# Mixing matmuls of an attention and gated-MLP kernel on float16 pairs in place of float32r pairs

## The chip, the cores and the metric

The kernel runs on one core of one Trainium2 chip. The metric is device time in microseconds for one launch. Before the change it is 624.42 us, the median of three runs (623.97 to 627.14).

The core has five engines that run their own instruction streams and meet at semaphores: TensorE (PE, with the weight loads shown apart as PEld), VectorE (DVE), ScalarE (ACT), GpSimd (POOL) and SyncE (SP), which issues the DMAs here.

## The reference

Two stages follow each other. The attention is causal with a window of 128, with a linear bias for each head; its heads are joined into x. The MLP splits its hidden layer in halves u and v, normalises v over its features, mixes v over the sequence with `w_spatial`, and multiplies the result into u.

```
B, H, S, D = 8, 8, 576, 64          # x: 8 x 576 x 512
scores = q @ k.T / sqrt(D) - slope[h] * |i - j|, kept where 0 <= i - j < 128
x = softmax(scores) @ v              # heads side by side
h = relu(x @ w_in)                   # 512 -> 1024
u, v = h[..., :512], h[..., 512:]
v_n = (v - mean(v)) / sqrt(var(v) + 1e-6)
v_s[b, t, d] = sum_s w_spatial[t, s] * v_n[b, s, d] + b_spatial[t]
out = (u * v_s) @ w_out              # 512 -> 512
```

`w_spatial` is 576 x 576 with normally distributed entries of size 0.64 / 576, and `b_spatial` lies around 1. All inputs and the output are float32.

## The kernel before

The work is held to 128 partitions. The sequence of 576 is four tiles of 128 and a rest of 64. Products that must be more exact than one pass are done on pairs: an operand is a high part plus a low part, and three matmuls add high x high, high x low and low x high (`PASS`).

For each of eight batches the attention makes x in four pairs of heads: scores on PE (L537), a fused bias and row minimum on VectorE (L548), the exponential on ACT (L554), then a split of the scaled probabilities into float16 high and low parts on ACT and VectorE (L589, L594), a DMA transpose, and float16 matmuls with v (L656). Some pairs at the start take another road with full float32 matmuls (`raw_tile`, `raw_rest`).

The MLP of a batch is made of units, each filling one PSUM tile `m`, of which there are two. Five v units (L721, and L743 for the rest of 64) make v: relu, `layer_norm`, then a split into `vn`, high and low. Eight u units (L773) make u transposed, relu'd. Eight mixing units (`sp_unit`, L794) multiply `vn` with the pairs `wsp` of the transposed mixing weights: twelve matmuls on whole tiles and two on the rest, where `l1`, `l2`, `r1`, `r2` hold the rest's high and low parts stacked, with the bias in two further rows. VectorE then multiplies the PSUM tile into u (L802), and the product is split again (`gs`). Eight output units (L820) multiply with `wout` and go out by DMA. The string `UORDER` sets the order of these kinds in a batch.

The order of the instructions on each engine is made by a planner (`Plan`). Every operation has an engine, a weight, a due time and the parts of buffers that it reads and writes; an `either` operation has two engines to choose from, and the planner takes the one that it reckons to be free first. Operations that are ready go out by due time. Because all engines share one plan, an added operation can move others and change which of ACT and VectorE gets an `either`. `copy` (L278) and `relu` (L282, L283) are such helpers, so their operations stand under the helper's line.

At the start the weights are prepared between the first batch's attention tiles: `win` and `wout` are split from float64 words by bit operations (`split_w64`, L297 to L335), and the mixing weights are split from float32 by `wsp_weights` (L365 to L373) and `rest_weights` (L382 to L404). The latter load into buffers `gs`, of which there are five; the splits of `win` use the same five for their steps.

Of the kernel before, what the change touches and what calls it, by code (L numbers as in the profile page):

```python
# [140 lines left out]
def attn_gmlp_kernel(ctx, tc, qk, v, w_in, w_spT, b_sp, w_out, outT):  # L141
# [14 lines left out]
    PSC = 4096.0  # L156
    VORDER = (0, 4, 1, 2, 3)
# [203 lines left out]
    def wsp_weights(c, due):  # L361
        st = plan.buf(work, "gs", 5, [P, S], F32)

        def f():
            nc.sync.dma_start(st(), w_spT[c * P:(c + 1) * P, :])  # L365
        plan.add("SP", dma(P * S * 4), due - 4000, f, (), [(st, 0)])

        def f():
            nc.scalar.copy(wsp()[:, c, 0, :], st())
        plan.add("ACT", act(S), due, f, [(st, 0)], [(wsp, (c, 0))])  # L370

        def f():
            nc.vector.tensor_tensor(wsp()[:, c, 1, :], st(), wsp()[:, c, 0, :].bitcast(F32), ALU.subtract)  # L373
        plan.add("DVE", dve(S), due, f, [(st, 0), (wsp, (c, 0))], [(wsp, (c, 1))])

    def rest_weights(due):
# [474 lines left out]
    for c in range(NQ - 1):  # L851
        wsp_weights(c, FIRST + 8000 + 2000 * c)
# [64 lines left out]
```

## Time and profile before

| | |
|---|---|
| time, median of three runs | 624.42 us (623.97 to 627.14) |
| span of the profiled execution | 625.2 us |
| mean granted TensorE clock | 0.985 |
| matmuls | 5388 |
| VectorE instructions counted | 1945 |
| ACT instructions counted | 1312 |

The page gives the span as the only time of the profiled execution; it is 0.8 us above the median and lies inside the runs. "Busy" counts the time in which at least one instruction of an engine was under way. Matmuls overlap their neighbours, so a matmul's mean is a latency and not its share of the time. A group names line, engine, operation, tiles written and read, shapes and count; then busy microseconds and mean nanoseconds of one; then the idle time just before its instructions, with what ended it. `x0`, `vn0` and the like lose their numbers in the views, so `m` stands for both PSUM tiles.

### The profile page before, as it was taken

What the parts mean: (1) busy time and instruction counts of PE and PEld (TensorE: products, weight loads), DVE (VectorE), ACT (ScalarE), POOL (GpSimd) and SP (SyncE); (2) the same over time, 40 slices, a digit from 0 to 9 for tenths busy, and PEclk for the clock granted to TensorE, in tenths of its full rate; (3) what the DMA queues carried; (4) which work ended last, traced back from release to release, by engine and by line L of the source; (5) the groups of instructions that cost most, each with busy time, mean ns of one, the idle gap of its engine ahead of it and who ended that gap; (6) DMA issues with size and microseconds to landing.
All of it is one profiled execution on the core that took longest, in us unless ns stands there. A gap on an engine that the chain in (4) does not pass through costs nothing. (4 is left out here: it accounts for less than half of the span.)

```text
span 625.2 us, 14903 instructions
## 1 busy us (share of the span) xinstructions
PE 591.6 (95%) x5388; PEld 521.6 (83%) x5388; DVE 536.7 (86%) x1945; ACT 422.7 (68%) x1312; POOL 30.0 (5%) x53
## 2 busy tenths in 40 slices
PE   4889899799899998999999999999999999999997
PEld 2446579689689987998899988998899889998997
DVE  7989888998998988998999999999999899984532
ACT  4678765897785775975597677877597568752211
POOL 1000010000100001000100001000200010000100
PEclk9979799989999999999999999999999999999999
DMA  7902113499746681587646872587557761671001
GB/s 262 348 23 86 63 68 102 136 187 218 148 100 140 145 206 60 116 151 181 140 120 121 190 171 81 121 190 174 127 116 157 176 118 35 93 140 45 0 23 54
DMA packets 153613, 80.27 MB, mean 128 GB/s; under 512 B 132930, under 2 KB 144194, under 8 KB 153540
## 3 DMA queue, kind: packets, MB, share of 16 engines
q1 hardware_dynamic: 153540, 79.32, 54.0%
q8 instruction: 42, 0.69, 0.5%
q14 instruction: 31, 0.25, 0.1%
HBM read 37.13 MB, written 9.44 MB: 74 GB/s over the span
## 5 line engine op out<-in xcount | busy, mean ns | idle before, releaser
L554 ACT ACTIVATE prob<-prob,stat 128x256 f32<-128x256 f32 (+2 forms) x270 | 125.3, 466 | 36.7 <-DVE stat L548 36.7
L794 PE MATMUL m<-wsp,vn 128*128 128x288 f32 x768 | 122.2, 299 | 3.8 <-DVE u L802 1.7
L773 PE MATMUL m<-xt,win 128*128 128x288 f32 x768 | 111.6, 298 | 4.2 <-DVE u L283 2.2
L794 PEld LDWEIGHTS m<-wsp,vn 128*128 128x128 f32 x768 | 107.0, 188 | 8.6 <-DVE u L802 2.8
L773 PEld LDWEIGHTS m<-xt,win 128*128 128x128 f32 x768 | 103.9, 188 | 9.5 <-DVE u L283 3.9
L820 PE MATMUL m<-gs,wout 128*128 128x288 f32 x768 | 110.3, 299 | 0.2 <-ACT o L278 0.2
L589 ACT ACTIVATE pq<-prob,stat 128x128 f16<-128x128 f32 x270 | 104.4, 466 | 7.4 <-ACT prob L554 2.4
L820 PEld LDWEIGHTS m<-gs,wout 128*128 128x128 f32 x768 | 103.5, 189 | 4.1 <-DVE gs L808 1.5
L594 DVE SCALAR_TENSOR_TENSOR pq<-prob,stat,pq 128x128 f16<-128x128 f32 x270 | 104.9, 435 | 1.7 <-ACT pq L589 0.9
L721 PE MATMUL m<-win,xt 128*128 128x512 f32 x384 | 92.9, 397 | 2.4 <-DVE vt L283 1.7
L721 PEld LDWEIGHTS m<-win,xt 128*128 128x128 f32 x384 | 72.3, 190 | 19.5 <-DVE vt L283 2.1
L548 DVE CUSTOM_DVE_ANT_0 prob<-s,tab 128x256 f32<-128x256 f32 (+2 forms) x222 | 75.0, 377 | 1.0
L691 POOL TENSOR_TENSOR st<-st,nhalf 128x1 f32<-128x1 f32 (+1 forms) x40 | 26.0, 652 | 538.1 <-DVE st L687 527.2
L554 ACT ACTIVATION_READ_ACCUMULATOR prob<-prob,stat 128x1 f32 (+1 forms) x270 | 50.8, 188 | 0.0
L802 DVE TENSOR_TENSOR u<-m,u 128x288 f32<-128x288 f32 x64 | 28.6, 449 | 25.5 <-PE m L794 25.1
L537 PE MATMUL s<-qkraw 64*64 64x192 f32 (+2 forms) x876 | 41.9, 316 | 2.9 <-DVE stat L548 2.9
L656 PE MATMUL x<-pt,vh 128*64 128x256 f16 (+6 forms) x756 | 42.0, 229 | 0.0
L537 PEld LDWEIGHTS s<-qkraw 64*64 64x64 f32 x876 | 30.9, 136 | 9.6 <-issue 4.8
L282 ACT ACTIVATE vt<-m 128x512 f32<-128x512 f32 x31 | 18.5, 595 | 27.8 <-DVE st L686 17.3
L656 PEld LDWEIGHTS <-vh 128*64 128x64 f16 x756 | 32.3, 110 | 4.8 <-issue 4.6
L656 PE MATMUL x<-pt,vl 128*64 128x256 f16 (+6 forms) x378 | 35.5, 228 | 0.0
L278 ACT COPY o<-m 128x288 f32<-128x288 f32 x36 | 14.1, 393 | 31.7 <-PE m L820 24.1
(132 smaller groups left out, 837.3 us busy)
## 6 DMA issues: line engine op xcount, KB each, us to landing
qkraw<-in_qk_dram SPq DMA_DIRECT2D x28, 576.0 KB, 4.2
out_dram<-o SPq DMA_DIRECT2D x64, 144.0 KB, 2.1
vraw<-in_v_dram SPq DMA_DIRECT2D x28, 320.0 KB, 3.0
vn<-in_w_in_dram SPq DMA_DIRECT2D x6, 512.0 KB, 6.8
pt<-in_w_out_dram SPq DMA_DIRECT2D x4, 512.0 KB, 4.3
gs<-in_w_spT_dram SPq DMA_DIRECT2D x4, 288.0 KB, 4.9
xt<-in_w_in_dram SPq DMA_DIRECT2D x2, 512.0 KB, 7.0
qkraw<-in_qk_dram SPq DMA_DIRECT2D x3, 320.0 KB, 9.0
```

What stands on the lines that cost most here:

```text
L537: nc.tensor.matmul(sc[k][j]()[out, i, a - k0:z - k0], raw()[rows, 0, q:q + D], raw()[rows, 1, a:z], start=True, stop=True, skip_group_chec ...
L548: nc.vector.tensor_tensor_reduce(pt(), sc()[:m, i, :n], tabs[h]()[:m, c0:c0 + n], -0.125, 3e38, ALU.add, ALU.min, st()[:m, NM, j, t:t + 1])
L554: nc.scalar.activation(pt(), pt(), AF.Exp, bias=st()[:m, NM, j, t:t + 1], scale=-1.0, accum_out=st()[:m, SM, j, t:t + 1])
L589: nc.scalar.activation(pq[j]()[:m, 0, cs], prob[j]()[:m, cs], AF.Copy, scale=st()[:m, RC, j, t:t + 1])
L594: nc.vector.scalar_tensor_tensor(pq[j]()[:m, 1, cs], prob[j]()[:m, cs], st()[:m, RC, j, t:t + 1], pq[j]()[:m, 0, cs], ALU.mult, ALU.subtract)
L656: nc.tensor.matmul(xp()[j * D:(j + 1) * D, x0:x0 + n], l()[:, kt, j * D:(j + 1) * D], rhs[:, o:o + n], start=j not in seen, stop=False, sk ...
L691: nc.gpsimd.tensor_tensor(st()[:m, 11:12], st()[:m, 10:11], nhalf()[:m], ALU.pow)
L721: nc.tensor.matmul(pt(), xt[c]()[:, X0[a] + t * P:X0[a] + (t + 1) * P], win()[:, c, w, DH:DF], start=(n == 0), stop=(n == 3 * NC_ - 1))
L773: nc.tensor.matmul(pt()[:, :HS], win()[:, c, w, d * P:(d + 1) * P], xt[c]()[:, X0[a] + hf * HS:X0[a] + (hf + 1) * HS], start=(n == 0), sto ...
L794: nc.tensor.matmul(pt()[:, :HS], l, r, start=(n == 0), stop=(n == len(ops) - 1))
L802: nc.vector.tensor_tensor(u(), pt()[:, :HS], u(), ALU.mult)
L820: nc.tensor.matmul(pt()[:, :HS], wout()[:, d, w, e * P:(e + 1) * P], gs[d]()[:, a, :], start=(n == 0), stop=(n == 3 * ND - 1))
```

## The change

Three groups of things change.

First, the tiles `wsp`, `r1`, `r2`, `l1`, `l2` and `vn` become float16. The pairs stay pairs: high part rounded to float16, low part the rounded remainder, and the same three products. The tile `vn` keeps its size in bytes, since the loads of `w_in` pass through it. PE's mixing matmuls read float16 on both sides.

Second, factors keep the float16 values in range. `layer_norm` multiplies the variance by 2048 to the power of -2, so v_n comes out 2048 times as large. The mixing weights and the bias are multiplied by a power of two that is found on the device from the largest row sum of absolute values: ACT takes absolute values of all weights with a running sum a partition, VectorE takes the largest of three sums, spreads it over 128 columns as bfloat16, a DMA transposes that, and `scale_of` reduces it and works on the exponent bits. The factor that undoes both goes into the gating multiply, which becomes `scalar_tensor_tensor`.

Third, the loads of the mixing weights go to a tile of their own, `wraw`, and `mixing_weights` takes the place of `rest_weights` and `wsp_weights`, with one due time of 8000 after `FIRST`. The splits read the factor, so they come after the scan.

```diff
+    VSC = 2048.0
-    wsp = fixed([P, NQ - 1, 2, S], F32R, "wsp")
-    r1 = fixed([P, S], F32R, "r1")
-    r2 = fixed([P, S], F32R, "r2")
-    l2 = fixed([P, DH], F32R, "l2")
+    wsp = fixed([P, NQ - 1, 2, S], F16, "wsp")
+    wraw = fixed([P, NQ - 1, S], F32, "wraw")
+    wam = fixed([P, 8], F32, "wam")
+    r1 = fixed([P, S], F16, "r1")
+    r2 = fixed([P, S], F16, "r2")
+    l2 = fixed([P, DH], F16, "l2")
...
+        for c in range(NQ - 1):
+            plan.add("SP", dma(P * S * 4), due - 4000 + c, lambda c=c: nc.sync.dma_start(wraw()[:, c, :], w_spT[c * P:(c + 1) * P, :]),
+                     (), [(wraw, c)])
...
+        def f():
+            nc.scalar.activation(flat(), wraw(), AF.Abs, accum_out=wam()[:, 0:1])
+            nc.scalar.activation(r1(), rs(), AF.Abs, accum_out=wam()[:, 1:2])
+            nc.scalar.activation(r2()[64:65], bt()[64:65], AF.Abs, accum_out=wam()[64:65, 2:3])
+        plan.add("ACT", act((NQ + 1) * S, 1) + 400, due, f, chunks + [(rs, 0), (bt, 0), (wam, 0), (r2, 2)],
+                 [(wsp, (c, 0)) for c in range(NQ - 1)] + [(wam, 1), (r1, 0), (r2, 1)])
...
+        def f():
+            nc.vector.tensor_reduce(wam()[:, 3:4], wam()[:, 0:3], AX.X, ALU.max)
+            nc.vector.tensor_copy(wide(0), wam()[:, 3:4].to_broadcast([P, P]))
+        plan.add("DVE", 300, due + 1, f, [(wam, 1)], small[0] + [(wam, 2)])
+        plan.add("SP", 300, due + 2, lambda: nc.sync.dma_start_transpose(out=wide(1), in_=wide(0)), small[0], small[1])
...
+            scale_of(wam, wide(1), 2.0 ** -13 / VSC)
...
+                nc.scalar.activation(wsp()[:, c, 0, :], wraw()[:, c, :], AF.Copy, scale=sc())
...
+                nc.vector.scalar_tensor_tensor(wsp()[:, c, 1, :], wraw()[:, c, :], sc(), wsp()[:, c, 0, :], ALU.mult, ALU.subtract)
...
+    def scale_of(am, rows, back):
+        bits = 0x7F800000
+        nc.vector.tensor_reduce(am()[:, 1:2], rows, AX.X, ALU.max)
+        nc.vector.tensor_scalar(am()[:, 2:3], am()[:, 1:2], 2.0 ** -98, 2.0 ** 126, ALU.max, ALU.min)
+        nc.vector.tensor_scalar(am()[:, 2:3].bitcast(I32), am()[:, 2:3].bitcast(I32), bits, None, ALU.bitwise_and)
+        nc.vector.tensor_scalar(am()[:, 5:6], am()[:, 2:3], 2.0 ** -12, None, ALU.mult)
+        nc.vector.tensor_scalar(am()[:, 6:7], am()[:, 2:3], back, None, ALU.mult)
+        nc.vector.tensor_scalar(am()[:, 5:6].bitcast(I32), am()[:, 5:6].bitcast(I32), bits, None, ALU.bitwise_xor)
...
-            nc.vector.tensor_scalar(st()[:m, 10:11], st()[:m, 9:10], 1e-6, None, ALU.add)
+            nc.vector.tensor_scalar(st()[:m, 10:11], st()[:m, 9:10], 1e-6, VSC ** -2, ALU.add, ALU.mult)
...
-        vn = [plan.buf(work, f"vn{t}", 1, [P, 2, DH], F32R) for t in range(NQ - 1)]
-        l1 = plan.buf(work, "l1", 1, [P, DH], F32R)
+        vn = [plan.buf(work, f"vn{t}", 1, [P, 2, 2 * DH], F16) for t in range(NQ - 1)]
+        l1 = plan.buf(work, "l1", 1, [P, DH], F16)
...
-                nc.vector.tensor_tensor(u(), pt()[:, :HS], u(), ALU.mult)
-            plan.add("DVE", dve(HS), due, f, [(pt, 0), (u, 0)], [(u, 0)])
+                nc.vector.scalar_tensor_tensor(u(), pt()[:, :HS], wam()[:, 6:7], u(), ALU.mult, ALU.mult)
+            plan.add("DVE", dve(HS), due, f, [(pt, 0), (u, 0), (wam, 3)], [(u, 0)])
...
-    rest_weights(FIRST + 6000)
-    for c in range(NQ - 1):
-        wsp_weights(c, FIRST + 8000 + 2000 * c)
+    mixing_weights(FIRST + 8000)
```

How this moves instructions shows at three places. The rows give line, operation, tiles and shape; lines of the changed kernel are 3 to 36 higher than the same lines before. `ISA` is the fused bias and row minimum of a score tile, `prob` the probabilities, `win` the split weights, `r` and `l` the rest's tiles.

On VectorE, in the start, the rest's and the first chunk's low parts stood singly between score tiles before:

```order
L447 ISA prob_88,rstat<-s_67,tab_78 128x256
L447 ISA rstat 128x1
L474 TENSOR_SCALAR prob_88<-prob_88,rstat 128x256
L447 ISA prob_87,rstat<-s_68,tab_79 128x256
L447 ISA rstat 128x1
L393 TENSOR_TENSOR r_85<-gs,r_84 64x576
L373 TENSOR_TENSOR wsp<-gs,wsp 128x576
L278 COPY pq_89<-m 128x512
L447 ISA prob_88,rstat<-s_69,tab_80 128x256
L447 ISA rstat 128x1
```

Now the reduction of the scan and the cast stand a few score tiles later, with four scalings of `prob` on VectorE behind them:

```order
L483 ISA prob_89,rstat<-s_68,tab_75 128x256
L483 ISA rstat 128x1
L399 TENSOR_REDUCE wam<-wam 128x1
L400 CAST wsp<-wam 128x128
L494 TENSOR_SCALAR rstat<-rstat 128x2x2
L495 RECIPROCAL rstat<-rstat 128x2x2
L510 TENSOR_SCALAR prob_89<-prob_89,rstat 128x256
L510 TENSOR_SCALAR prob_90<-prob_90,rstat 128x256
L510 TENSOR_SCALAR prob_89<-prob_89,rstat 128x256
L510 TENSOR_SCALAR prob_90<-prob_90,rstat 128x256
```

The reduction L399 waits for ACT's scan, and all that follows in VectorE's queue stands behind it. `scale_of` (L437 to L442) comes some twenty operations later, and the low parts of the weights behind that.

On ACT the scan is three activations in one place, between exponentials (`prob,rstat`):

```order
L488 ACTIVATE prob_90,rstat<-prob_90,rstat 128x256
L281 COPY pq_92<-m 128x512
L390 ACTIVATE wsp,wam<-wraw 128x4x576
L391 ACTIVATE r_86,wam<-gs 128x576
L392 ACTIVATE r_87,wam<-gs 1x576
L488 ACTIVATE prob_90,rstat<-prob_90,rstat 128x256
```

Before, the casts of the mixing weights stood singly among other work:

```order
L452 ACTIVATE prob_88,rstat<-prob_88,rstat 128x256
L452 ACTIVATE prob_87,rstat<-prob_87,rstat 128x256
L369 CAST wsp<-gs 128x576
L278 CAST xt<-x 128x128
L473 ACTIVATE prob_88<-prob_88,rstat 128x256
L369 CAST wsp<-gs 128x576
```

The scan holds ACT from its first activation to its last, and the exponentials of later score tiles come after it.

On SP, which issues the loads, the mixing weights stood behind a `w_in` load, in `gs` buffers:

```order
L356 DMA pt<-in_w_out_dram 128x1024
L343 DMA vn_254<-in_w_in_dram 128x1024
L382 DMA gs<-in_w_spT_dram 64x576
L383 DMA gs<-in_w_spT_dram 64x576
L384 DMA gs<-in_b_sp_dram 1x576
L385 DMA gs<-in_b_sp_dram 1x576
L365 DMA gs<-in_w_spT_dram 128x576
L343 DMA vn_272<-in_w_in_dram 128x1024
L365 DMA gs<-in_w_spT_dram 128x576 x3
```

Now they stand ahead of the `w_out` and `w_in` loads, and a transpose is new:

```order
L369 DMA wraw<-in_w_spT_dram 128x576 x4
L359 DMA pt<-in_w_out_dram 128x1024
L346 DMA vn_261<-in_w_in_dram 128x1024
L374 DMA gs<-in_w_spT_dram 64x576
L375 DMA gs<-in_w_spT_dram 64x576
L376 DMA gs<-in_b_sp_dram 1x576
L377 DMA gs<-in_b_sp_dram 1x576
L346 DMA vn_277<-in_w_in_dram 128x1024
L402 DMA_TRANSPOSE wsp<-wsp 128x128
```

The rest and the bias kept their place and their `gs` buffers. On PE the order of the units is the same from the middle of the first batch's mixing on.

More of the change, by code (lines that the diff above doesn't have):

```diff
@@ L359, in wout_weights, with mixing_weights @@
         split_w64((st, DM), (wout, (c,)), tmp, lambda: wout()[:, c, 0, :], lambda: wout()[:, c, 1, :], due, WPE[2])
[L361 to L376, printed above, removed]
+    def mixing_weights(due):
         rs, bt = (plan.buf(work, "gs", 5, [P, S], F32) for _ in range(2))
+        chunks = [(wraw, c) for c in range(NQ - 1)]
+        for c in range(NQ - 1):
+            plan.add("SP", dma(P * S * 4), due - 4000 + c, lambda c=c: nc.sync.dma_start(wraw()[:, c, :], w_spT[c * P:(c + 1) * P, :]),
+                     (), [(wraw, c)])
         def f():
@@ L385, in f @@
             nc.sync.dma_start(bt()[96:97, :], b_sp)
-        plan.add("SP", 2000, due - 4000, f, (), [(rs, 0), (bt, 0)])
+        plan.add("SP", 2000, due - 3900, f, (), [(rs, 0), (bt, 0)])
         def f():
-            nc.scalar.copy(r1(), rs())
-        plan.add("ACT", act(S), due, f, [(rs, 0)], [(r1, 0)])
-        def f():
-            nc.vector.tensor_tensor(r2()[0:R, :], rs()[0:R, :], r1()[0:R, :].bitcast(F32), ALU.subtract)
-        plan.add("DVE", dve(S), due, f, [(rs, 0), (r1, 0)], [(r2, 0)])
+            nc.gpsimd.memset(wam(), 0.0)
+            nc.gpsimd.memset(r2()[R:P, :], 0.0)
+            nc.gpsimd.memset(l2()[R:P, :], VSC)
@@ new lines, in mixing_weights @@
+        plan.add("POOL", 1500, 0, f, (), [(wam, 0), (r2, 2), (l2, 1)])
+        flat = lambda: wsp()[:, :, 0, :]
+        def f():
+            nc.scalar.activation(flat(), wraw(), AF.Abs, accum_out=wam()[:, 0:1])
[3 more added lines that the diff above has]
+                 [(wsp, (c, 0)) for c in range(NQ - 1)] + [(wam, 1), (r1, 0), (r2, 1)])
@@ L396, in f @@
+        wide = lambda k: wsp()[:, 1 + k, 1, 0:P].bitcast(BF16)
+        small = [[(wsp, (1 + k, 1))] for k in range(2)]
         def f():
-            nc.gpsimd.memset(r2()[R:P, :].bitcast(F32), 0.0)
-            nc.gpsimd.memset(l2()[R:P, :].bitcast(F32), 1.0)
-        plan.add("POOL", 1500, due, f, (), [(r2, 2), (l2, 1)])
+            nc.vector.tensor_reduce(wam()[:, 3:4], wam()[:, 0:3], AX.X, ALU.max)
+            nc.vector.tensor_copy(wide(0), wam()[:, 3:4].to_broadcast([P, P]))
+        plan.add("DVE", 300, due + 1, f, [(wam, 1)], small[0] + [(wam, 2)])
@@ new lines, in mixing_weights, with f @@
+        plan.add("DVE", 600, due + 3, f, [(wam, 2), *small[1], (powers, 0)], [(wam, 3)])
+        sc = lambda a=0, z=P: wam()[a:z, 5:6]
+        ready = [(wam, 3)]
+        for c in range(NQ - 1):
+            def f(c=c):
+                nc.scalar.activation(wsp()[:, c, 0, :], wraw()[:, c, :], AF.Copy, scale=sc())
+            plan.add("ACT", act(S, 1), due + 10 + c * 500, f, [(wraw, c)] + ready, [(wsp, (c, 0))])
+            def f(c=c):
+                nc.vector.scalar_tensor_tensor(wsp()[:, c, 1, :], wraw()[:, c, :], sc(), wsp()[:, c, 0, :], ALU.mult, ALU.subtract)
+            plan.add("DVE", dve(S), due + 20 + c * 500, f, [(wraw, c), (wsp, (c, 0))] + ready, [(wsp, (c, 1))])
@@ L761, in f @@
             def f():
[L762 removed]
+                nc.vector.tensor_tensor(l1()[R:2 * R], vt()[0:R], l1()[0:R], ALU.subtract)
             plan.add("DVE", dve(DH), due + 6, f, [(vt, 0), (l1, 0)], [(l1, 1)])
```

18 lines of the change are left out of this document (11 added, 7 removed).

## The prediction

> **What bounds the kernel now.** I read the page's first part, then the stages, then the waits of each engine in one steady batch, then the order of time around one mixing unit.
>
> ```profile
> PE 591.6 (95%) x5388; PEld 521.6 (83%) x5388; DVE 536.7 (86%) x1945; ACT 422.7 (68%) x1312; POOL 30.0 (5%) x53
> ```
>
> These means hide the stages. Columns of the next view: stretch, length, busy time of PE, PEld, DVE, ACT and POOL, granted clock, DMA share, GB/s.
>
> ```profile
> 22.00:50.00 28.00, 23.44 (x166) 13.91 (x165) 25.12 (x99) 21.34 (x69) 0.00 (x0) 0.88 0.38 119
> 50.00:98.00 48.00, 45.09 (x277) 33.15 (x278) 44.17 (x143) 37.19 (x109) 3.90 (x5) 0.93 0.21 71
> 98.00:154.00 56.00, 51.36 (x554) 45.82 (x553) 49.14 (x198) 43.09 (x147) 1.00 (x2) 0.97 0.71 167
> 154.00:226.00 72.00, 69.20 (x673) 61.89 (x672) 66.07 (x247) 54.71 (x172) 2.78 (x5) 1.00 0.65 148
> ...
> 298.00:366.00 68.00, 67.63 (x675) 62.25 (x675) 64.31 (x238) 50.71 (x162) 3.25 (x5) 1.00 0.65 147
> ...
> 502.00:568.00 66.00, 65.64 (x636) 60.48 (x635) 57.17 (x203) 43.77 (x134) 3.25 (x5) 1.00 0.53 94
> 568.00:625.20 57.20, 53.93 (x364) 51.18 (x363) 22.64 (x55) 11.14 (x24) 2.83 (x5) 0.99 0.08 27
> ```
>
> There are three regimes. Up to 98 us VectorE is the fuller of the two elementwise engines and nearly full itself: from 22 to 98 us it idles 2.9 + 3.8 = 6.7 us. From 98 to 502 us PE and VectorE are both nearly full. From 502 us on VectorE has room and PE alone sets the pace. PE's busy time counts overlapping ends, so for the middle regime I ask who waits: PE from 226 to 568 us, then VectorE in one batch, 298 to 366 us (total us, times, longest).
>
> ```profile
> PE m L773 <- DVE u L283: 2.2, 5, 0.7
> PE m L794 <- ACT o L278: 1.7, 2, 0.9
> PE m L773 <- ACT vt L282: 1.7, 2, 1.1
> PE m L721 <- DVE o L278: 0.6, 1, 0.6
> ```
>
> ```profile
> DVE stat L577 <- ACT prob L554: 0.6, 3, 0.2
> DVE vt L752 <- ACT vt L278: 0.4, 1, 0.4
> DVE u L802 <- PE m L794: 0.4, 1, 0.4
> DVE prob L548 <- PE x L537: 0.3, 1, 0.3
> DVE st L682 <- ACT vt L282: 0.2, 1, 0.2
> ```
>
> PE waits 6.2 us in 342: it sets the pace. But VectorE waits only 1.9 us in 68, and of these 1.3 trace back to PE (0.4 and 0.3 directly, 0.4 and 0.2 through ACT's copy out of a PE tile); the other 0.6 is a loop between VectorE and ACT. So the second engine stands about one microsecond behind the first in every batch, and what is taken from PE soon meets it.
>
> **The change part by part.** *The mixing matmuls.* There are 768 + 128 = 896, 112 in a batch:
>
> ```profile
> L794 PEld LDWEIGHTS m<-wsp,vn 128*128 128x128 f32 x768 | 107.0, 188 | 8.6 <-DVE u L802 2.8 <-ACT o L278 2.1 <-issue 1.4
> ...
> L794 PEld LDWEIGHTS m<-r,l 128*128 128x128 f32 x128 | 20.5, 188 | 0.0
> ```
>
> Each has one weight load of 188 ns, which runs under the matmul before. The pace is read off the order of time (start, length, engine, line, count):
>
> ```profile
> 331.59 1.64 PEld L773 LDWEIGHTS m<-xt,win 128*128 128x128 f32 x12
> ```
>
> ```profile
> 335.53 1.24 PEld L794 LDWEIGHTS m<-wsp,vn 128*128 128x128 f32 x9
> ```
>
> Twelve loads make (1.64 - 0.188) / 11 = 132 ns per matmul, and the nine mixing ones (1.24 - 0.188) / 8 = 131.5. Float16 matmuls occur in the attention, two heads side by side:
>
> ```profile
> 331.71 1.74 PE L773 MATMUL m<-xt,win 128*128 128x288 f32 x12
> 333.38 0.41 PE L656 MATMUL x<-pt,vh 128*64 128x256 f16 x4
> ...
> 334.16 0.36 PE L656 MATMUL x<-pt,vh 128*64 128x224 f16 x4
> ...
> 334.45 0.33 PE L656 MATMUL x<-pt,vh 128*64 128x192 f16 x4
> ...
> 334.70 0.23 PE L656 MATMUL x<-pt,vh 128*64 128x64 f16 x4
> ```
>
> Three pairs of 224 columns take 334.45 - 334.16 = 0.29 us, 96.7 ns each; three of 192 take 0.25, 83.3 each. That is 0.42 ns a column and 2.9 over, so 288 columns come to 123.5 ns. The trace has no float16 weights of 128 columns at this tile, so the price is bounded: 123.5 from the rows of the same type, 132 from the rows of the same tile. I take 123.5, because what differs from column count alone (0.42 ns x 288 = 121) is 2.9 ns there against 11 here and goes with the type as far as rows show. The gain is 8.5 ns a matmul, 0.95 us a batch, 7.6 us in all. The Trainium skill (TensorE: Matmul & The Clock Gate, Back-to-back issue gap) gives N/2.4 + 2.5 ns for an isolated warm matmul; by it 288 columns take an estimated 122.5 ns and the total gain would be 8.5 us. The float16 rows follow it (95.8 for 224 columns against 96.7), the float32r rows do not.
>
> *What of that arrives.* From 502 us on, two batches' worth, all of it: 2 x 0.95 = 1.9 us. In the middle VectorE sets the limit. It can give up at most the 1.3 us that trace to PE, and it gets work: the gating multiply becomes a form with a per-partition factor, which I price by the same form out of PSUM.
>
> ```profile
> L669 DVE SCALAR_TENSOR_TENSOR xt<-x,am,xt 128x288 fp32r<-128x288 f32 x54 | 25.5, 503 | 3.8 <-ACT xt L665 3.8
> ...
> L802 DVE TENSOR_TENSOR u<-m,u 128x288 f32<-128x288 f32 x64 | 28.6, 449 | 25.5 <-PE m L794 25.1
> ```
>
> Eight a batch at 503 - 449 = 54 ns add 0.43 us. So a middle batch gains between -0.4 (no wait shortens) and 1.3 - 0.43 = 0.87 us. I take 0.55: PE has two PSUM tiles for these units and cannot run far ahead. Four batches give 2.2. The first two, where VectorE idles 6.9 and 5.9 us (98 to 226 us), I set at 0.5 each, since there the idle time lies in a few long waits. Together 1.9 + 2.2 + 1.0 = 5.1 us. The float16 results of VectorE and ACT I cost at nothing: the operations, element counts and float32 inputs stay.
>
> *The start.* The factor for the mixing weights needs a scan of all of them on ACT, a reduction, a transpose by DMA and a chain of small operations. The order also shows that the planner answers by moving work from ACT to VectorE. Ahead of the first gating multiply VectorE has six more scalings of 256 columns, one fewer of 192, three more casts of `win` from `gs`, one fewer from `m`, two more casts of `xt`, two fewer copies of `pq`, and the new chain.
>
> ```profile
> L278 DVE COPY pq<-m 128x512 f32<-128x512 f32 x6 | 4.0, 683 | 0.1
> L474 DVE TENSOR_SCALAR prob<-prob,rstat 128x256 f32<-128x256 f32 x12 | 3.6, 347 | 0.0
> ...
> L474 DVE TENSOR_SCALAR prob<-prob,rstat 64x192 f32<-64x192 f32 x6 | 1.7, 304 | 0.0
> ...
> L278 DVE CAST xt<-x 128x128 fp32r<-128x128 f32 x5 | 1.4, 287 | 1.8 <-PE x L501 1.7
> ...
> L278 DVE CAST win<-m 128x512 fp32r<-128x512 f32 x2 | 1.4, 684 | 0.0
> ...
> L278 DVE CAST win<-gs 128x512 fp32r<-128x512 f32 x3 | 1.3, 426 | 0.1
> ```
>
> ```profile
> L628 DVE TENSOR_REDUCE am<-vl 128x1 f32<-128x128 bf16 x27 | 7.4, 275 | 4.1 <-DMA vl<-vl 3.9
> ...
> L619 DVE CAST vl<-am 128x128 bf16<-128x128 f32 x27 | 6.5, 245 | 0.1
> ...
> L629 DVE TENSOR_SCALAR am<-am 128x1 f32<-128x1 f32 x27 | 4.2, 154 | 0.9
> ```
>
> 6 x 0.347 - 0.304 + 3 x 0.426 - 0.684 + 2 x 0.287 - 2 x 0.683 = 1.58 us. The chain is a cast, a reduction and six short operations, 0.245 + 0.275 + 6 x 0.154 = 1.44, and the four low halves of the weights take the dearer form, 4 x 0.05 = 0.2: together 3.2 us on the engine that is nearly full there. I charge all of it; the bounds are 0 (its 6.7 idle us swallow it) and the two stalls below. ACT comes out about even: the scan (four times 576 elements a partition, then 576 twice) against six scalings and the casts.
>
> ```profile
> L612 ACT ACTIVATE vl<-vraw 128x640 f16<-128x640 f32 x27 | 19.7, 730 | 0.0
> ...
> L473 ACT ACTIVATE prob<-prob,rstat 128x256 f32<-128x256 f32 x18 | 8.3, 504 | 0.8 <-DVE rstat L459 0.8
> ```
>
> At 730 ns for 640 elements the scan is at most 0.73 x 3456 / 640 = 3.9 us; the scalings return 6 x 0.504 = 3.0 and the casts the rest. But the scan is one block: the exponentials queue behind it on ACT, and VectorE's reduction waits for its end with everything after that in VectorE's queue. The score reductions ahead of it cover part; bare it would cost 3.9 us. The DMA transpose has some twenty VectorE operations between its two ends; bare it would cost its landing time:
>
> ```profile
> vl<-vl SPq DMA_TRANSPOSE x27, 2.3
> ```
>
> The four loads of mixing weights move ahead of one `w_out` and one `w_in` load on SP's queue and no longer wait for `gs` buffers; the DMA engines are 0.38 busy from 22 us on. I cost that at nothing; if `w_out` and `w_in` ran late for it, splitting those weights would be late next. POOL gets one short memset.
>
> Sum: 625.2 - 5.1 + 3.2 = 623.3 us of span. The profiled span is 0.8 above the median of 624.42, so the forecast is **622.5**.
>
> **The rivals.**
> *PE paces everything and the start is swallowed.* For it: PE waits 6.2 us in 342; VectorE idles 6.7 us before 98. Against: those idle stretches are waits inside chains, and VectorE's margin is 1.3 us a batch. Seven batches at 0.9 to 0.95 and a partial first: 7.0 us, 617.4.
> *VectorE is the bound up to 502 us.* This is the one on the other side. Nothing of PE's gain arrives before the last two batches, and each added VectorE operation lengthens the program: 3.2 + 6 x 0.43 - 1.9 = +3.9, 628.3. For it: 64.31 of 68.00 busy. Against: VectorE still waits for PE at the end of every batch's mixing. It decides if fewer than 0.43 of the 1.3 us can be had back; the bare stalls at the start would act the same way.
> *The matmuls do not get faster.* Either 128 float16 weight columns keep the 132 ns, or PE drains when the type changes within a tile. A change of tile costs that today: the twelfth L773 matmul starts at 331.71 + 11 x 0.132 = 333.16, the next at 333.38, 0.09 us late. The order has seven boundaries a batch between mixing and other units of the same tile; 56 x 0.09 = 5.0 of the 7.6 us would go. Two thirds of the rest, 1.7, against 3.2 gives 625.9; with no gain at all 627.6. The Trainium skill's same section puts a stream of weight loads and matmuls of 128 columns at 81 ns, 25 over the isolated one; by that a mixing matmul would take an estimated 148 ns and the kernel lose some 14 us. The rows at 132 ns with loads of 188 speak against it, so it has 2 in 100 of this rival's share.
>
> **How the numbers follow.** The forecast has 0.45 (its own range 619.5 to 625.5), PE everywhere 0.22, VectorE everywhere 0.18, no faster matmuls 0.15. A measurement here can tell about 0.5%, 3.1 us, from no change: faster means below 621.3, slower above 627.5. Faster: 0.22 and 0.15 of the forecast; slower: 0.13 of the VectorE rival, 0.07 of the last and 0.01 of the forecast; the rest, 0.42, is no change that can be told. The range of 615 to 629 takes in the full PE gain with some of the start's moved loads helping, and VectorE as the bound.
>
> **What would show it.** The mixing loads' pace: 123.5 ns right, 132 wrong. At boundaries of equal tile the first matmul no later than today. Per batch from 226 to 502 us: VectorE's waits for PE down from 1.3 towards 0.3, PE's waits for VectorE up. The first gating matmul of L773 some 3 us later, with VectorE 3 us busier before it. The last batch 0.95 us shorter. The forecast falls if VectorE before 98 us does not get longer, or if middle batches shorten by a full 0.95 or not at all.

## The result

The kernel after takes 629.26 us in the median of 17 runs (627.32 to 633.26), the kernel before 625.71 us beside it (623.46 to 628.24). The ratio is 1.0050, with an interval of 1.0033 to 1.0068: 0.5% slower, where 622.5 us and no change or a small gain were forecast. The profiled execution of after has a span of 631.5 us; it is the slowest of its 17 runs, 4.0 us above their median, at a granted clock of 0.976, where the six runs at 0.986 to 0.989 took 627.3 to 628.2 us.

Busy time and the stages of the kernel after (the page's first part; then some of the stretches shown for before, with the same columns: stretch, length, busy time of PE, PEld, DVE, ACT and POOL, granted clock, DMA share, GB/s):

```profile
PE 590.2 (93%) x5388; PEld 494.2 (78%) x5388; DVE 543.0 (86%) x1963; ACT 425.0 (67%) x1308; POOL 29.7 (5%) x54
```

```profile
22.00:50.00 28.00, 22.55 (x146) 14.83 (x148) 23.10 (x94) 21.66 (x66) 0.00 (x0) 0.80 0.35 121
50.00:98.00 48.00, 42.91 (x255) 30.88 (x252) 44.07 (x147) 33.11 (x95) 2.99 (x4) 0.87 0.21 71
98.00:154.00 56.00, 51.63 (x498) 42.09 (x497) 50.80 (x194) 42.28 (x133) 1.94 (x3) 0.94 0.62 145
...
298.00:366.00 68.00, 66.86 (x672) 57.78 (x671) 63.61 (x234) 49.84 (x160) 3.25 (x5) 1.00 0.67 146
...
502.00:568.00 66.00, 63.96 (x631) 55.52 (x629) 61.52 (x222) 47.10 (x148) 3.25 (x5) 1.00 0.53 98
```

The first three rows are the news: before 154 us PE runs fewer matmuls than before at a lower granted clock (0.80, 0.87 and 0.94, against 0.88, 0.93 and 0.97). Two rows of the order of time cut the program in two: the first matmul of the u units (L773 before, L809 after), which the prediction calls the first gating matmul, of before and then of after.

```profile
87.55 1.75 PE L773 MATMUL m<-xt,win 128*128 128x288 f32 x12
```

```profile
93.64 5.22 PE L809 MATMUL m<-xt,win 128*128 128x288 f32 x36
```

Up to that matmul after loses 6.1 us. From it to the end before takes 625.2 - 87.55 = 537.7 us and after 631.5 - 93.64 = 537.9. So in this execution nothing at all is left of the faster mixing, although the mixing itself is faster. (The two profiled spans are 6.3 us apart, the medians 3.6.) Weight loads of before stand in the prediction; of after, a stretch of one batch in the order of time:

```profile
336.24 1.08 PEld L830 LDWEIGHTS <-vn 128*128 128x128 f16 x9
```

One load takes 98 ns now (188 before), so nine make (1.08 - 0.098) / 8 = 123 ns a matmul. Over the neighbouring mixing matmuls of the whole trace (starts less than 150 ns apart) the mean is 122.8 ns after and 132.4 before, 9.6 ns less. The Trainium skill (TensorE: Matmul & The Clock Gate, Back-to-back issue gap) gives N/2.4 + 2.5 ns for an isolated matmul, an estimated 122.5 for 288 columns: the trace agrees for float16. The change of type costs nothing that shows here either. The next rows hold the same 54 matmuls, 42 of them mixing, with three changes of type in after, from the first row's start to the last one's, of before and of after:

```profile
324.48 0.67 PE L794 MATMUL m<-wsp,vn 128*128 128x288 f32 x3
...
328.03 0.55 PE L794 MATMUL m<-wsp,vn 128*128 128x288 f32 x3
...
331.71 1.74 PE L773 MATMUL m<-xt,win 128*128 128x288 f32 x12
```

```profile
330.64 0.54 PE L830 MATMUL m<-wsp,vn 128*128 128x288 f16 x3
...
334.04 0.53 PE L830 MATMUL m<-wsp,vn 128*128 128x288 f16 x3
...
337.37 0.92 PE L809 MATMUL m<-xt,win 128*128 128x288 f32 x5
```

From the first start to that of the last row it is 7.23 us before and 6.73 after. That last start is no good mark, for in after it comes 28 ns behind its neighbour's and the next one 228 ns later. To the second matmul of the last row the trace gives 7.37 and 6.96 us: 0.41 us less, 9.7 ns for each of the 42, which is the pace alone. Where it goes in the middle batches is seen in PE's waits from 226 to 568 us of after:

```profile
PE m L856 <- DVE u L838: 2.6, 5, 0.7
PE m L809 <- DVE u L286: 1.6, 5, 0.7
PE m L830 <- ACT o L281: 1.5, 2, 1.3
PE m L809 <- ACT vt L285: 1.1, 1, 1.1
PE m L830 <- DVE o L281: 1.0, 1, 1.0
```

The row at the head is new. The output units (L856) now stand and wait for VectorE's gating multiply, a wait that no row of before shows; PE reaches them sooner and VectorE has not finished.

The start shows more than one stall. PE's longest waits from 22 to 98 us, VectorE's wait for the scan, the scan on ACT, and two stretches inside PE's longest wait with the granted clock (the last column but two), all of after:

```profile
PE m L519 <- DVE prob L510: 3.6, 1, 3.6
PE s L477 <- DVE rstat L483: 2.2, 3, 1.3
PE x L537 <- DVE xt L545: 2.0, 2, 1.6
```

```profile
DVE wam L399 <- ACT r L392: 1.6, 1, 1.6
```

```profile
41.81 2.12 ACT L390 ACTIVATE wsp<-wraw 128x2304 f16<-128x2304 f32 x1
...
45.31 0.18 ACT L392 ACTIVATION_READ_ACCUMULATOR r<-gs 1x1 f32 x1
```

```profile
43.40:45.40 2.00, 0.05 (x2) 0.00 (x0) 0.52 (x3) 1.98 (x6) 0.00 (x0) 1.00 0.00 0
45.50:47.00 1.50, 0.00 (x0) 0.00 (x0) 1.16 (x6) 1.48 (x6) 0.00 (x0) 0.50 0.00 0
```

The scan holds ACT from 41.81 to 45.49 us, 3.7 us. The exponentials stand behind it, VectorE waits 1.6 us for it, and PE then waits 3.6 us for a scaling that stands behind that. PE stands from 43.45 to 47.07 us, and inside this wait the granted clock falls to 0.50, between 45.4 and 45.5 us. The Trainium skill (TensorE: Matmul & The Clock Gate, Part 1: The HAM clock gate) says that the clock is halved after an idle window of about 3.4 us; here it fell some 2.0 us into the wait, so the rows do not show such a window. The kernel before loses its clock at 40.4 us, and the 3.4 us ahead of that hold 1.57 us of PE work and no wait over 1.9 us:

```profile
37.00:40.40 3.40, 1.57 (x10) 1.13 (x10) 3.33 (x12) 2.63 (x9) 0.00 (x0) 1.00 0.33 87
42.00:46.00 4.00, 4.00 (x24) 2.36 (x22) 3.04 (x14) 2.68 (x9) 0.00 (x0) 0.50 0.00 0
```

So the clock can fall without one long stall, while PE is thinly fed; what share of work keeps it up these rows do not tell. Where a late VectorE brings such a fall, it is paid for twice, once as a wait and once as slower matmuls.

### The profile page after: what moved, and what is told of

Read it like the earlier page. It is cut to its first block, busy times and chain, and to the rows that moved or that the text cites. A ratio compares the mean times of both kernels' runs of the same rounds, so it can differ in the third digit from the quotient of the medians.

```text
span 631.5 us, 14922 instructions
## 1 busy us (share of the span) xinstructions
PE 590.2 (93%) x5388; PEld 494.2 (78%) x5388; DVE 543.0 (86%) x1963; ACT 425.0 (67%) x1308; POOL 29.7 (5%) x54
## 5 line engine op out<-in xcount | busy, mean ns | idle before, releaser
L856 PE MATMUL m<-gs,wout 128*128 128x288 f32 x768 | 115.3, 304 | 3.6 <-DVE u L838 2.6
L809 PE MATMUL m<-xt,win 128*128 128x288 f32 x768 | 113.9, 301 | 3.3 <-DVE u L286 1.6
L830 PE MATMUL m<-wsp,vn 128*128 128x288 f16 x768 | 112.0, 286 | 5.1 <-DVE u L838 1.9
L856 PEld LDWEIGHTS m<-gs,wout 128*128 128x128 f32 x768 | 105.5, 191 | 10.0 <-DVE u L838 4.1
L809 PEld LDWEIGHTS m<-xt,win 128*128 128x128 f32 x768 | 103.8, 189 | 9.5 <-DVE u L286 3.4
L757 PE MATMUL m<-win,xt 128*128 128x512 f32 x384 | 95.1, 402 | 2.9 <-DVE o L281 1.4
L830 PEld LDWEIGHTS <-vn 128*128 128x128 f16 x768 | 72.7, 98 | 27.5 <-issue 8.5
L838 DVE SCALAR_TENSOR_TENSOR u<-m,wam,u 128x288 f32<-128x288 f32 x64 | 32.5, 509 | 21.3 <-PE m L830 21.3
L718 DVE BATCH_NORM_STATS2 st<-vt 128x6 f32<-128x512 f32 (+1 forms) x40 | 27.3, 687 | 9.7 <-ACT vt L285 9.7
```

Of the source, the lines that this page charges most:

```text
L718: nc.vector.bn_stats(st()[:m, 0:6], vt()[:m])
L757: nc.tensor.matmul(pt(), xt[c]()[:, X0[a] + t * P:X0[a] + (t + 1) * P], win()[:, c, w, DH:DF], start=(n == 0), stop=(n == 3 * NC_ - 1))
L809: nc.tensor.matmul(pt()[:, :HS], win()[:, c, w, d * P:(d + 1) * P], xt[c]()[:, X0[a] + hf * HS:X0[a] + (hf + 1) * HS], start=(n == 0), sto ...
L830: nc.tensor.matmul(pt()[:, :HS], l, r, start=(n == 0), stop=(n == len(ops) - 1))
L838: nc.vector.scalar_tensor_tensor(u(), pt()[:, :HS], wam()[:, 6:7], u(), ALU.mult, ALU.mult)
L856: nc.tensor.matmul(pt()[:, :HS], wout()[:, d, w, e * P:(e + 1) * P], gs[d]()[:, a, :], start=(n == 0), stop=(n == 3 * ND - 1))
```

## The experiments

Every kernel ran beside the kernel before on the same chip, whose median was then 625.8 to 626.7 us; kernels are compared by their ratios to it. 0.1% is 0.6 us.

**Types alone, factor alone, both.** In before.py the six tiles are made float16 and nothing else (e1); the gating multiply alone gets a per-partition factor of one (e2); both (e4). The orders are those of the kernel before.

```diff
-    wsp = fixed([P, NQ - 1, 2, S], F32R, "wsp")
+    wsp = fixed([P, NQ - 1, 2, S], F16, "wsp")
...
-    nc.vector.tensor_tensor(u(), pt()[:, :HS], u(), ALU.mult)
+    nc.vector.scalar_tensor_tensor(u(), pt()[:, :HS], back(), u(), ALU.mult, ALU.mult)
```

> The kernel before with the tiles of the mixing operands in float16 and nothing else: no factors, no scan, the old loads and splits, so the order of every engine is the one before. If PE paces the middle, the 8.5 to 11 ns saved on each of 896 matmuls arrive almost whole: 7 to 9 us faster, about 617.5. If VectorE sets the pace up to 502 us, only the last two batches gain: 2 us faster, about 623.7. The forecast's own middle way says 5 us, 620.6. If switching types at the same tile costs, no gain at all.

> The kernel before, in float32r, with only the gating multiply changed to the form with a per-partition factor (of 1). If VectorE sets the pace up to 502 us: 6 x 0.43 = 2.6 us slower, about 628.3. If PE paces and VectorE's 1.9 us of waits a batch take it up: 0 to 0.5 us slower, about 626.

> The float16 tiles and the gating multiply with a factor (of 1) together, in the old start. If PE's gain and VectorE's loss meet in the middle batches, this is slower than the types alone by up to 2.6 us more than the two effects alone add up to; under the forecast it is 625.7 - 5.1 = 620.6, and under VectorE as the bound 625.7 + 2.6 - 1.9 = 626.4.

Measured: e1 622.96 us, ratio 0.9945 (0.9924 to 0.9966); e2 626.98, 1.0012 (0.9995 to 1.0028); e4 622.80, 0.9950 (0.9931 to 0.9970). The types are worth 3.4 us, the dearer multiply nothing that can be told, alone or with the types. (The tile of the factor of one also moves every later tile of e2 and e4 by 32 bytes. Against h2 below, with work tiles at the same place, e2 stands 0.3% higher, so a cost of up to some 2 us is not excluded.) What loses in after lies in the rest of the change, the preparation of the weights and the order that comes with it: after stands 1.0050 - 0.9950 = 1.0%, 6.3 us, behind e4. In the two profiled executions it is 6.2 us behind at the first gating matmul (93.64 against 87.48) and 3.7 more at the end, at a lower clock; the second part was not traced to a cause.

**The changed kernel without the scan.** Here the scan, the reduction, the transpose and the search for the factor are left out and constants written instead; the own tile, the due times and the loads stay.

```diff
-            nc.scalar.activation(flat(), wraw(), AF.Abs, accum_out=wam()[:, 0:1])
...
+            nc.vector.memset(wam()[:, 5:6], 16.0)
+            nc.vector.memset(wam()[:, 6:7], 2.0 ** -4 / VSC)
```

> The changed kernel with its two factors as constants: the scan on ACT, the reduction, the transpose by DMA and the exponent chain are gone, all else stays (own tile and early loads for the weights, one due time, splits with a factor, gating with a factor). If the scan and what hangs on it cost the start its time, the end of the start comes some 4 to 5 us earlier: about 624.5. If the start is late because work moved from ACT to VectorE and the loads moved, it stays within 1.5 us of the changed kernel: 628 to 629.5.

Measured: 632.47 us, ratio 1.0101 (1.0077 to 1.0124), slower than after. The stall behind the scan is real in after's trace, but taking the scan away brings nothing: the order that the planner makes without it is nearly as late at the start (first gating matmul at 92.2 us).

**What in the start is late.** Four kernels change the order of the weights' preparation. f4 is e1 with the raw mixing weights in a tile of their own, and nothing else of the change. j1 is f4 with ring buffers held, so that the `w_in` splits cannot come early. f2 is after with the `w_in` splits held back behind the mixing splits. f6 is after with the raw weights back in the ring and the remainder and the bias in an own tile, at the tile places of f1 (below).

```diff
 f4  -        st = plan.buf(work, "gs", 5, [P, S], F32)
     +        st = lambda: wraw()[:, c, :]
 j1  +        held = plan.buf(work, "gs", 5, [P, S], F32)
     +        plan.add("POOL", 60, due, lambda: nc.gpsimd.memset(held()[:, 0:8], 0.0), [(wsp, (c, 1))], [(held, 0)])
 f2  -            win_weights(0, c, UDUE[c], w_u[c])
     +            win_weights(0, c, UDUE[c], w_u[c], [(wsp, (c, 1))])
 f6  -        rs, bt = (plan.buf(work, "gs", 5, [P, S], F32) for _ in range(2))
     +        wraw = [plan.buf(work, "gs", 5, [P, S], F32) for _ in range(NQ - 1)]
```

> Float16 types alone (e1_types), with only one more thing: the four loads of mixing weights go to a tile of their own instead of the ring gs of five buffers. No factors, no scan, the loads at the places where e1_types has them. Theory 'the ring': the buffers that the mixing loads leave free let the planner put the first w_in split at 15 score reductions instead of 29, and that alone costs most of the 6 us: 626.5 to 629 (ratio 1.001 to 1.005). Rival 'the early loads and the bunching of the mixing splits': as e1_types, 623 (0.9945).

> f4_own (float16 types, mixing loads in a tile of their own), but each mixing chunk also holds one buffer of the ring gs until its low half is written, by an 8-column memset on POOL that waits for it. The first w_in split of the u columns is then at 29 score reductions in VectorE's order, as in e1_types (f4_own: 15), the second at 32; the mixing splits stay early (17 to 21). Theory 'the early w_in split': most of the 5 us between f4_own and e1_types comes back: 623 to 625 (ratio 0.995 to 0.998). Rival 'the early mixing splits, or early loads, do it': as f4_own, 627.7 (1.0026).

> The kernel after, with each w_in split of the u columns made to wait for the low half of one mixing chunk, so that all four come at 32 score reductions in VectorE's order (after: the first at 15; before: 29, 32, 40, 43). Theory 'the start is slow because the first of these splits runs early, ahead of what v units and attention need': most of the 6 us that after stands behind types and factor alone comes back: 623.5 to 626. Rival 'the early mixing loads or the factor's chain themselves': no change, 629. The four splits now stand in a bunch, which may cost 1 to 2 us by itself.

> The kernel after with the alignment of f1_align, and with the raw mixing weights back in four buffers of the ring gs while the remainder and the bias get the own tile; the scan is six reads instead of three. The splits of w_in's u columns then find no free buffers early: in VectorE's order all four come at 32 score reductions, with the mixing splits. Theory 'own tile and free ring make the start late': the first u unit comes earlier than the 93.2 us of f1_align, by 2 to 4 us, and the time is 620 to 622.5. Rival 'the wait for the factor makes the start late, whatever the ring': first u unit at 93 us or later, 624 to 626.

Measured: f4 627.73 us, ratio 1.0026 (1.0009 to 1.0043); j1 628.72, 1.0061 (1.0034 to 1.0088); f2 629.74, 1.0059 (1.0037 to 1.0081); f6 623.84, 0.9948 (0.9930 to 0.9967). The work up to the first gating matmul, from one window each that ends there, of e1, of f4 and of after (columns as in the stages above):

```profile
0.00:85.20 85.20, 68.25 (x402) 43.39 (x403) 76.08 (x280) 60.93 (x185) 5.34 (x14) 0.96 0.47 156
```

```profile
0.00:93.00 93.00, 74.52 (x410) 47.99 (x410) 78.78 (x288) 64.35 (x186) 6.21 (x15) 0.91 0.43 143
```

```profile
0.00:93.60 93.60, 73.35 (x402) 48.16 (x402) 80.39 (x292) 62.12 (x179) 5.87 (x16) 0.87 0.42 142
```

f4 shows it without factor, scan or chain: the own tile alone costs 1.0026 - 0.9945 = 0.8%, 5.1 us. The loads are then off the ring `gs`, the planner finds free buffers and runs the first `w_in` split at 15 score reductions instead of 29 and the mixing splits at 19 to 24 instead of 23 to 32. The first gating matmul comes 7.8 us later than in e1, with 2.7 us more VectorE work before it, 5.1 us more VectorE idle, and 0.91 of the clock instead of 0.96. A part of that is the clock: the kernel before, in e1's order at 0.92, is only 5.5 us ahead of f4, and f4's six runs at 0.984 to 0.986 have a median of 627.1 us against 623.8 of e1's five at 0.985 to 0.986.

Late loads are not the reason, for in f4 no engine's wait from 22 to 98 us is for a DMA. What grows is PE's waiting for the attention's score reductions (`rstat`) and probabilities (`prob`), here of e1 and then of f4:

```profile
PE s L441 <- DVE rstat L447: 2.2, 2, 1.9
PE s L483 <- ACT prob L473: 1.3, 1, 1.3
PE m L483 <- ACT prob L473: 1.0, 1, 1.0
```

```profile
PE s L442 <- DVE rstat L448: 3.3, 3, 1.3
PE s L484 <- ACT prob L474: 2.2, 1, 2.2
PE m L484 <- ACT prob L474: 1.9, 2, 1.2
```

These make 4.5 us in e1 and 7.4 in f4; the same waits make 8.9 in j1 and 8.5 in e3, whose mixing splits also come early. That the early splits push the attention's work back is the likely reading, but no run moves that work alone.

My narrower theory, that the early `w_in` split is the culprit, fell with j1: there the ring buffers are held and the first split is back at 29, the mixing splits stay early (17 to 21), the last two `w_in` splits come at 32 and 35 instead of 40 and 43, and it is as slow. It fell with f2 too, where all four `w_in` splits come at 32. Every order tried here but the one that the kernel before happens to have puts the first gating matmul at 91.7 to 96.1 us (84.7 to 87.6 with that order). f6, with the raw weights in the ring again, has the first gating matmul at 96.1 us and the time of f1, whose places it has (0.9948 and 0.9965, the intervals overlap). Its order has the mixing splits at 32 score reductions, behind the reduction for the factor at 28, so there the wait for the factor probably holds them. It reaches that matmul 2.9 us later than f1 and makes up for it afterwards, so the time of this matmul alone is no price. Which single wait of these orders costs most is left open.

**Who paces the middle batches.** In g1 the subtraction for the low half of `gs` on top of e1 is a copy of u, which leaves that correction out and saves VectorE 0.156 us (454 to 298 ns) eight times a batch in the same order; g2 does the same to the kernel before.

```diff
-                nc.vector.tensor_tensor(gs()[:, 1, :], u(), gs()[:, 0, :].bitcast(F32), ALU.subtract)
+                nc.vector.tensor_copy(gs()[:, 1, :], u())
```

> Float16 types alone (e1_types), and the subtraction that makes the low half of gs is replaced by a copy of u, which leaves the correction of that half out and takes some 304 instead of 455 ns: 0.15 us x 8 = 1.2 us less for VectorE in each batch, at the same place in the same order. Theory 'with float16 VectorE sets the pace of the middle batches, 1 to 6': each of them gets 0.6 to 1.2 us shorter, 4 to 7 us in all, 616 to 619. Rival 'TensorE still sets it': under 2 us in all, 621 to 623.

> The kernel before, with the subtraction for the low half of gs replaced by a copy of u (304 instead of 455 ns; the correction of that half is left out), as in g1_e1low: VectorE gets 1.2 us less in each batch. Control: if TensorE sets the pace of the kernel before, this brings under 2 us (624 to 626, ratio 0.997 to 1.000), against the 4.2 us that it brought on top of the float16 types. If VectorE sets the pace here as well, it brings 4 us or more (622, 0.993).

Measured: g1 618.73 us, ratio 0.9876 (0.9846 to 0.9906), against e1's 0.9945: 4.3 us. g2 622.61, 0.9933 (0.9913 to 0.9954): 4.2 us. The control was meant to show nothing and shows as much. So VectorE paced the kernel before as well, or more exactly: 64 x 0.156 = 10.0 us less VectorE work bring 4.2 us, and 896 x 9.6 ns = 8.6 us less PE work (e1) bring 3.4. The two engines hand the path to and fro, and here either one's gain arrives by some 40%. In e1 PE's waits from 226 to 568 us already show the row that after has, and which before has not:

```profile
PE m L773 <- DVE u L283: 2.2, 5, 0.7
...
PE m L820 <- DVE u L802: 1.6, 5, 0.6
```

**The place of the tiles.** Types and own tile do not close the account. The small tile for the factors is 32 bytes a partition and lies before all work tiles, so these moved by an odd half of 64 bytes against `win`. Six kernels change only where the work tiles lie, by the width of that tile or of an unused one; their order of instructions is that of the kernel that they start from, but for one short memset. i4 is i1 with the output copies on ACT.

```diff
 f1  -    wam = fixed([P, 8], F32, "wam")        i3  +    wam = fixed([P, 32], F32, "wam")
     +    wam = fixed([P, 16], F32, "wam")
 h1, h2  +    pad = fixed([P, 8], F32, "pad")    i1, i2, i4  +    pad = fixed([P, 16], F32, "pad")
 i4  -            copy(HS, lambda: (o(), pt()[:, :HS]), due, [(pt, 0)], [(o, 0)])
     +            plan.add("ACT", act(HS), due, lambda: nc.scalar.copy(o(), pt()[:, :HS]), [(pt, 0)], [(o, 0)])
```

> The kernel after, with the small tile for the factors 64 bytes a partition wide instead of 32, so that xt starts at a multiple of 64 bytes again, as win does; the order of instructions is that of after. Theory 'the two operands 32 bytes apart modulo 64 slow the 512-column float32r matmuls': their pitch is back from 234 to 229 ns, the o units' from 134 to 132, and of at most 480 x 5 ns + 768 x 2 ns = 3.9 us of TensorE time some part arrives: 625.5 to 629.3. Rival 'the clock granted, not the address, made the difference': pitch stays 234, time as after (629.3).

> Float16 types alone (e1_types) plus one unused tile of 32 bytes a partition behind the mixing weights, so that xt, gs, vn and the rest start at 32 modulo 64 bytes while win, wout and wsp stay at 0, as in after. The order of instructions is that of e1_types but for one short memset at the start. Theory 'the 32 bytes between the operands': the pitch of the v units goes from 229 to 234 ns and the time rises by as much as the alignment gave back in f1_align, 5 us: 626 to 629 (ratio 1.000 to 1.005). Rival 'f1_align was faster for another reason': 623 (0.9945).

> The kernel before (float32r pairs) with the same unused tile of 32 bytes a partition, so that the work tiles start at 32 modulo 64 bytes and win, wout and wsp at 0. Theory 'the 32 bytes between the operands slow TensorE's float32r matmuls': TensorE sets the pace here, so the time rises by at least the 480 x 5 ns = 2.4 us of the v units, and by 4 to 7 if the other units with win and wout go the same way: 628.5 to 633 (ratio 1.004 to 1.011). Rival: no change, 626.

> Float16 types alone (e1_types) plus an unused tile of 64 bytes a partition behind the mixing weights, so that every later tile lies 64 bytes further; the order is that of e1_types but for one short memset. In f1_align and f6_ring, whose work tiles also lie at 64 modulo 128 bytes where win lies, the DMA transposes of pq landed in 4.1 and 4.3 us (5.0 elsewhere) and the v units ran at 227 ns. Theory 'the place modulo 128 bytes is a gain of its own, no part of the change's loss': transposes at 4.1 to 4.4, pitch 227, and 3 to 5 us less than e1_types: 617.5 to 620 (ratio 0.986 to 0.990). Rival 'f1_align only took back a loss that the change had brought': as e1_types, 623 (0.9945).

> The kernel before with the same unused 64 bytes, in the same order of instructions. Theory 'a gain of its own': transposes at 4.1 to 4.4 us, pitch of the v units 227, 621 to 623.5 (ratio 0.991 to 0.996). Rival 'only the changed kernel suffered': 626 (1.000). If the transposes stay at 5.0, then not the place modulo 128 bytes decides but one modulo 512 (448 in f1_align and f6_ring, 192 here).

> The kernel after with the small tile for the factors 128 bytes a partition wide instead of 32 (f1_align had 64): the work tiles then lie 64 bytes from win modulo 128, as in before and e1_types. Order as in after. Theory 'place modulo 128': transposes back at 5.0 us, pitch 229, and the time between after and f1_align, nearer to after: 627 to 629.5 (ratio 1.002 to 1.006). The start of after, with its place as in before, then stands 4 to 6 us behind types and factor alone. Rival 'a multiple of 64 bytes is enough': as f1_align, 624 (0.9965).

> i1_e1pad64, and the copies of the output tiles out of PSUM are all put on ACT, where the planner now gives half of them to VectorE (four of 444 ns in a batch). Theory 'VectorE and TensorE share the path in the middle batches': up to 1.8 us a batch less for VectorE, worth 2 to 5 us in all beside i1_e1pad64: 614 to 617. Rival 'ACT's queue becomes late instead, or the planner answers by giving VectorE other work': no gain or a loss of up to 3 us, 618 to 622.

| kernel | starts from | start of `pt` modulo 128 bytes | pitch of 512-column float32r matmuls, ns | us to landing of `pt<-pq` | time, us | ratio (interval) |
|---|---|---|---|---|---|---|
| before | | 0 | 229 | 5.0 | 625.71 | 1 |
| h2 | before | 32 | 234 | 4.9 | 626.01 | 0.9982 (0.9965 to 0.9999) |
| i2 | before | 64 | 227 | 4.2 | 622.37 | 0.9939 (0.9917 to 0.9962) |
| e1 | types | 0 | 229 | 4.8 | 622.96 | 0.9945 (0.9924 to 0.9966) |
| h1 | e1 | 32 | 234 | 5.0 | 620.36 | 0.9894 (0.9874 to 0.9914) |
| i1 | e1 | 64 | 227 | 4.1 | 616.80 | 0.9841 (0.9816 to 0.9866) |
| after | | 32 | 234 | 5.1 | 629.26 | 1.0050 (1.0033 to 1.0068) |
| i3 | after | 0 | 233 | 5.1 | 628.73 | 1.0044 (1.0024 to 1.0064) |
| f1 | after | 64 | 227 | 4.1 | 624.14 | 0.9965 (0.9944 to 0.9986) |

f1 came first and misled me: it was 5 us faster than after, and I read that as 32 bytes of misalignment which the change had brought. h1 and h2 took that reading down. They have the misalignment and the pitch of 234 ns, and are no slower than the kernels they start from. The next kernels separated a loss from a gain: i2 gives the place of f1 to the kernel before and i1 to e1, and both gain (3.8 and 6.5 us); i3 gives the changed kernel the place modulo 128 that before has, and it stays at 1.0044. So the place is no part of the change's loss: at equal places the rest of the change loses 1.0 to 1.2% (i3 against e1, f1 against i1). It is a gain of 0.6 to 1.0% that lay open to the kernel before all along. What changes with it are the DMA transposes, here of after and of f1 (count, median us from issue to landing), and VectorE's waits behind the smaller ones, from the waits of the whole span, of after, of f1 and of before:

```profile
pt<-pq SPq DMA_TRANSPOSE x54, 5.1
```

```profile
pt<-pq SPq DMA_TRANSPOSE x54, 4.1
```

```profile
DVE am L664 <- DMA vl<-vl: 4.7, 5, 1.9
```

```profile
DVE am L664 <- DMA vl<-vl: 1.0, 1, 1.0
```

```profile
DVE am L628 <- DMA vl<-vl: 3.9, 5, 2.4
```

In i4 the output copies on ACT cost 9.6 us beside i1 (626.44 us, ratio 1.0002, 0.9983 to 1.0021): the rival had the direction, with a third of the size. PE's longest wait from 226 to 568 us is then for ACT's copy to free a PSUM tile:

```profile
PE m L721 <- ACT o L827: 6.4, 4, 1.6
```

i1, with float16 pairs, no factors, the ring as before and 64 unused bytes, beats both kernels: 616.8 us, 1.6% under before. Without factors the float16 pairs have no guard on their range.

## Why the prediction was wrong, point by point

*The mixing matmuls.* Right: 123.5 ns were taken, 122.8 measured; the other bound, 132, and the drain at a change of type did not come. The rival with no faster matmuls is out, and so is the estimate of 148 ns that the prediction worked out from the 81 ns of the Trainium skill (TensorE: Matmul & The Clock Gate, Back-to-back issue gap) for a stream with 128 columns.

*What of that arrives.* 5.1 us were forecast, 3.4 arrived (e1). By the starts of the remainder's v units (L743) in the order of time, e1 is 1.4 us shorter than before over the first two batches (1.0 forecast), 1.2 over the four middle ones (2.2, with the dearer multiply taken off) and 1.3 over the last two (1.9). The step that was wrong here is the reading of who waits. VectorE's 1.3 us a batch behind PE were taken as the room that is left. The better reading would have been that 64.31 of 68.00 us on VectorE and 67.63 on PE leave no room on either. g2 shows that less VectorE work sped up the kernel before, too. PE's waits (6.2 us in 342, of them 2.8 for VectorE and 3.4 for ACT) say how often PE was late, not how far PE's own length sets the time.

*The u multiply.* 54 ns a piece were nearly right (509 ns against 447 in e1, so 62), its 0.43 us a batch were not seen: with or without the types the form adds nothing that can be told (1.0012, and 0.9950 against 0.9945). The rival "VectorE is the bound up to 502 us" came close to the result with 628.3 us, but by luck: its 6 x 0.43 did not come, its 3.2 for the start was too small, and some gain did arrive in the middle.

*The start.* This is the step that failed. The row of before that ends at its first gating matmul stands against the one of after shown above:

```profile
0.00:87.50 87.50, 70.68 (x402) 44.78 (x403) 76.59 (x280) 61.36 (x185) 5.34 (x14) 0.92 0.45 152
```

The 3.2 us of added VectorE work was nearly right: 80.39 - 76.59 = 3.8 us up to the first gating matmul. I charged that work alone and moved the matmul by 3 us; it moved by 6.1, because VectorE also idled 2.3 us more (13.2 against 10.9), with PE's clock at 0.87 instead of 0.92. The sentence that went wrong is "The four loads of mixing weights ... no longer wait for `gs` buffers ... I cost that at nothing". That removal alone costs 5.1 us (f4). It acts through the planner's order, but not by the freed ring alone: j1 holds the ring and stays slow, with the mixing splits still early. Which of the moves costs it stays open. The order showed the moves, and I priced them as a sum of durations where they changed what PE waits for (4.5 us in e1, 7.4 in f4). The two stalls named at the side, 3.9 us for the scan and 2.3 for the transpose, were not charged; the first is in the trace (3.6 us of PE), but e3 shows that it is no separate term.

*The sum.* With the measured terms: 625.7 - 3.4 (types) + 0 (multiply) + 5.1 (own tile) = 627.4; 1.9 us to 629.3 are left for scan, chain and due times together, which no run took apart and which are about what the intervals of after and f4 leave uncertain. Against the kernel before, 1.9 us of gain were forecast and 3.6 us of loss came. Of the 5.5 us between them 1.7 are the gain that did not arrive (3.4 for 5.1), and 3.8 are the start (7.0 for 3.2). That the time missed the range of 615 to 629 by only 0.3 us is chance, for the kernel before was itself 1.3 us slower beside after than when the range was set. No case of the range held the larger start together with the smaller gain.

## What to carry to other kernels

Two engines that are busy for 95% and 99% of a stage can share its path, and then a gain on either arrives by a part only, here by some 40%; a control that relieves the other engine in the unchanged kernel tells how large a part. Taking a load out of a shared ring of buffers is a change of order, and must be priced by what the new order makes the busiest engines wait for, above all at a start where PE is thinly fed and also loses its clock. And before a small loss is explained by the change, the same shift of addresses belongs into the unchanged kernel.

## What the hardware showed

The DMA transposes of `pq` landed in 4.1 to 4.3 us in the five kernels here whose work tiles start at 64 modulo 128 bytes (f1, f6, i1, i2, i4), and in 4.8 to 5.1 in the fourteen at 0 or 32. The packets of 256 bytes, which are all the transposes, took some 165 us of each DMA engine in the first and 190 in the second, at the same count (168 in f1, 189 in after). All work tiles shift together here, and `pq` with them, so which of them matters is not known.

The 512-column float32r matmuls ran at 227, 229, 233 or 234 ns, in the same order of instructions, as the work tiles were moved against `win`: eight weight loads of one group in before, in after and in f1, all at clock 1.00, lasted

```profile
229.21 1.79 PEld L743 LDWEIGHTS m<-win,xt 128*128 128x128 f32 x8
```

```profile
236.25 1.82 PEld L779 LDWEIGHTS m<-win,xt 128*128 128x128 f32 x8
```

```profile
234.46 1.77 PEld L779 LDWEIGHTS m<-win,xt 128*128 128x128 f32 x8
```

which is (1.79 - 0.188) / 7 = 229, 233 and 226 ns. h1 and h2 show that it cost no time here. No rule follows: at 64 bytes from `win` modulo 128 before has 229 and i3 has 233. That h1 was faster than e1 (0.9894 against 0.9945) goes with the granted clock: its four runs had 0.989 to 0.992, e1's eight mostly 0.986, and e1's one run at 0.992 took 620.7 us, where h1's three took 620.3 to 620.8.
